# A fused top-k attention and two-stage mixture kernel: the float64 weights of the last stage are converted and split once into SBUF

## The chip, the cores and the metric

The kernel runs on one core of a Trainium2 chip. The metric is the device time of one execution in microseconds (us); lower is better. Three executions of the kernel before took 807.14, 808.33 and 810.57 us.

## The reference

```python
# attention: q, k, v are (2, 8, 576, 64), float32
scores = q @ k.T / sqrt(64)                       # 576 x 576 per batch and head
kth    = the 32nd largest score of each row       # top_k = 32
attn   = softmax of the scores >= kth, the rest left out
x      = (attn @ v), laid out as 1152 x 512       # batch and sequence by heads and head_dim

# first mixture: 4 experts, w1 (4, 512, 1024), w2 (4, 1024, 512), float32
p   = domain_probs / (domain_probs.sum(-1) + 1e-9)
out = sum over e of p[:, e] * (relu(x @ w1[e]) @ w2[e])

# second stage: w1, w2, w3 (512, 768), w_out (768, 512), float64
h      = max(out @ w1, out @ w2, out @ w3)
result = (h @ w_out).astype(float32)              # 1152 x 512
```

The four weights of the second stage are handed in as float64, as pairs of 32-bit words.

## The kernel before

The 1152 tokens are nine tiles of 128 rows, in four chunks of 2, 2, 2 and 3 tiles. `PHASES` runs the first mixture for chunks 0 to 3 and then the second stage for chunks 0 to 3. The attention makes the chunks' inputs one after another, and its work is woven into the first mixture of the earlier chunks: an outer loop steps through the attention's slots, and after each step `advance()` writes out matmul work until an estimate of TensorE's time (`clock["pe"]`) has reached a goal that grows with an estimate of VectorE's. So the program order is fixed when the kernel is written out; on the chip each engine works through its own queue in that order.

All matrix products use numbers split into two float32r parts, a high one and the rest (`product`: three matmuls for each pair of tiles). A weight of 128x1024 numbers is a unit. `w_load_to` loads it on SP's queue into one of three places `raw`; `w_split_to` (L225, L229) makes `hi` on ScalarE and `lo` by a subtraction on GpSimd, or, from chunk 3 on, on GpSimd and VectorE in turn. `hi` and `lo` have five places each, and a unit is split four units ahead of its use (`W_AHEAD`). A chunk of the first mixture uses 32 units: for each of 8 steps i, two units of the first layer (`half1`; PSUM is read by ScalarE and, L668, by VectorE) and two of the second (`half2`; the sum over experts, `acc`, is kept by VectorE, L697). `half2` of step i stands after `half1` of step i+1 in TensorE's queue. The outputs of `half2` have two PSUM places (pool `po`), so the third tile of a step can begin when VectorE has taken the first.

A chunk of the second stage uses 12 units: nine for the three first layers (`largest`, L791 keeps the maximum) and three for `w_out` (names `pso`). Before, each float64 unit is converted in four pieces of 128x256 (`to_float32`): two passes on ScalarE (L196, L197), three on VectorE (L199, L202, L205), an integer addition on GpSimd (L208), and a DMA on ScalarE's queue (L213) to a float32 copy in DRAM, `narrow`. These 48 pieces begin when the attention's slots end, one every two steps (`W_STEP`), and run beside the first mixture of chunk 3. From then on the second stage treats `narrow` like any float32 weight: for every chunk each unit is loaded and split anew, 48 loads and 48 splits. `turned` transposes a chunk's `acc` for the second stage (L745, L750, L751).

The pools of the attention (`kv`, `qp`, `at`) stay open to the end; chunk 3's hidden layer and sums take places of `kv` and `qp`.

Of the kernel before, what the change touches and what calls it, by code (L numbers as in the profile page):

```python
# [10 lines left out]
F32 = mybir.dt.float32  # L11
F32R = mybir.dt.float32r
# [7 lines left out]

# [10 lines left out]
WIDE, W_FROM, W_STEP = 4, 306, 2  # L31
# [19 lines left out]
def kernel(  # L51
# [43 lines left out]
    ms = ctx.enter_context(tc.tile_pool(name="ms", bufs=2))  # L95
    pg = ctx.enter_context(tc.tile_pool(name="pg", bufs=6, space=PSUM))
# [35 lines left out]
    def w_units():  # L132
# [21 lines left out]
        for part, c in PHASES:  # L154
            yield from (first if part == 1 else second)(c)

    dr = ctx.enter_context(tc.tile_pool(name="dr", bufs=1, space=bass.MemoryType.DRAM))
    wide = [((j, i), m[j]) for j in range(FF2 // 256) for i, m in enumerate((m1, m2, m3))]
    wide += [(j, mo[j]) for j in range(FF2 // 256)]
    narrow = {}  # L160
    for n, (key, _) in enumerate(wide):
        narrow[key] = dr.tile([P, 1024], F32, name="narrow%d" % n)
    narrow_at = {key if isinstance(key, tuple) else (key,): n for n, (key, _) in enumerate(wide)}
    narrowed = [0]
# [5 lines left out]
    def w_load_to(n):  # L170
        while w_pos["load"] < min(n, len(order)):
            key, src = order[w_pos["load"]]
            if key[1] in "cd" and narrowed[0] < WIDE * (narrow_at[key[2:]] + 1):
                return
# [5 lines left out]
    wide_raw = {}  # L180

    def wide_load(n):
        if n < WIDE * len(wide):
            wide_raw[n] = at.tile([P, 2048 // WIDE], U32, tag="s0", bufs=AHEAD_S, name="raw64")
            nc.sync.dma_start(out=wide_raw[n], in_=wide[n // WIDE][1][:, n % WIDE * 2048 // WIDE:(n % WIDE + 1) * 2048 // WIDE])

    def to_float32(n):
# [10 lines left out]
        yield True  # L198
        nc.vector.scalar_tensor_tensor(out=hf, in0=out, scalar=LEAST, in1=hf, op0=ALU.is_ge, op1=ALU.mult)  # L199
        dve(1024 // WIDE)  # L200
        yield True
        nc.vector.tensor_scalar(out=t, in0=high, scalar1=3, scalar2=0x3FFFFFF8, op0=ALU.logical_shift_left, op1=ALU.bitwise_and)  # L202
        dve(512 // WIDE)
        yield True
        nc.vector.scalar_tensor_tensor(out=t, in0=high, scalar=0xC0000000, in1=t, op0=ALU.bitwise_and, op1=ALU.bitwise_or)  # L205
        dve(1024 // WIDE)
        yield True
        nc.gpsimd.tensor_tensor(out=out.bitcast(I32), in0=out.bitcast(I32), in1=last, op=ALU.add)  # L208
        yield True
        yield True  # L210
        wide_load(n + AHEAD_S)
        yield True
        nc.scalar.dma_start(out=narrow[wide[n // WIDE][0]][:, n % WIDE * 1024 // WIDE:(n % WIDE + 1) * 1024 // WIDE], in_=out)  # L213
        narrowed[0] = n + 1

    def w_split_to(n):
        while w_pos["split"] < min(n, len(order)):
# [9 lines left out]
            late = w_pos["split"] - w_index[PHASES[LATE][1], "c" if PHASES[LATE][0] == 2 else "a", 0, 0]  # L227
            on = nc.vector if late >= 0 and late % 2 else nc.gpsimd
# [6 lines left out]
    def weight(key, oldest=None):  # L235

        w_split_to(w_index[oldest or key] + W_AHEAD)
        return w_hl[key]
# [237 lines left out]
    def attention():  # L476
# [69 lines left out]
        while s <= end:  # L546
# [20 lines left out]

# [347 lines left out]
```

## Time and profile before

| | us |
|---|---|
| median of three runs | 808.33 |
| the profiled execution, its own time | 808.2 |
| its span, first to last instruction | 806.4 |
| TensorE busy | 746.3 (93%) |
| VectorE busy | 683.8 (85%) |
| GpSimd busy | 527.2 (65%) |
| ScalarE busy | 492.7 (61%) |

The profile is of one execution. Its span leaves 1.8 us outside (808.2 against 806.4). PE is TensorE, DVE VectorE, ACT ScalarE, POOL GpSimd, SP SyncE. A row of the timeline has the start, the duration, the engine, the line of the kernel, the operation, the tiles it writes and reads, their shapes, and in brackets the idle time before it with what ended it. PE's durations overlap, since matmuls are pipelined: the distance from one start to the next is what a matmul costs.

### The profile page before, as it was taken

To read this page: it belongs to the slowest core of one execution; us is meant where nothing else is said; L and a number is where in the kernel's file an instruction comes from. 1 tells how busy PE (TensorE), PEld (TensorE's weight loads), DVE (VectorE), ACT (ScalarE), POOL (GpSimd) and SP (SyncE) were. 2 spreads that over 40 slices of the span, in tenths; PEclk is the share of its full clock that TensorE was granted. 3 is DMA by queue.
4 is the path that set the end of the run, shared out by engine and by line. 5 is a ranking of instruction groups with operands and counts; after the bars stand their busy time and mean duration, and the time that the engine had idled before them with its cause. 6 is when DMAs were issued, how large, how long until landed. Compare 5 with 4: busy or idle time off the path is not lost.

```text
span 806.4 us, 13973 instructions
## 1 busy us (share of the span) xinstructions
PE 746.3 (93%) x4942; PEld 663.2 (82%) x4942; DVE 683.8 (85%) x1242; ACT 492.7 (61%) x1027; POOL 527.2 (65%) x316
## 2 busy tenths in 40 slices
PE   3776799999999989999999999989999898999998
PEld 2454699888898879888888987879988697989996
DVE  6999989999999999999999996999999683445441
ACT  5666768677776775766777665665565444545541
POOL 2787968779888876668777685566565473555330
PEclk8556599999999999999999999999999899999999
DMA  3430245636545445253534364877777455656531
GB/s 98 117 106 13 68 131 147 190 117 173 174 137 171 135 146 151 88 169 112 161 126 146 112 188 152 270 249 250 245 251 243 157 178 167 232 165 208 178 102 40
DMA packets 50214, 126.24 MB, mean 157 GB/s; under 512 B 7904, under 2 KB 18144, under 8 KB 50144
## 3 DMA queue, kind: packets, MB, share of 16 engines
q1 hardware_dynamic: 41936, 116.69, 46.8%
q10 hardware_dynamic: 8208, 8.65, 3.1%
q8 instruction: 39, 0.64, 0.3%
q14 instruction: 31, 0.25, 0.1%
HBM read 116.67 MB, written 8.65 MB: 155 GB/s over the span
## 4 chain that ended last, share of the span: by engine, by line
DVE 41%; PE 35%; DMA 8%; issue 6%; POOL 4%; ACT 4%; SPq 2%; ACTq 0%; DVEq 0%; POOLq 0%
DVE m L370 14%; DVE work L372 13%; PE ps L588 9%; PE ps L590 9%; PE ps L589 9%; DVE p L390 6%; DMA narrow<-narrow 3%; POOL wlo L229 2%; DMA raw<-in_w_dram 2%; DVE h L668 2%; ACT whi L225 2%; SPq L246 2%; DMA kraw<-in_k_dram 1%; PE pso L590 1%; PE pso L588 1%
## 5 line engine op out<-in xcount | busy, mean ns | idle before, releaser
L229 POOL TENSOR_TENSOR wlo<-raw,whi 128x1024 fp32r<-128x1024 f32 x136 | 336.5, 2487 | 162.6 <-ACT whi L225 155.8
L225 ACT ACTIVATE whi<-raw 128x1024 fp32r<-128x1024 f32 x176 | 182.9, 1058 | 73.7 <-DMA raw<-narrow 23.8
L588 PE MATMUL ps<-xl,whi 128*128 128x256 f32 (+1 forms) x512 | 155.3, 303 | 1.7 <-DVE h L668 0.8
L370 DVE MAX8 m<-work 128x8 f32<-128x576 f32 x216 | 154.6, 742 | 0.1
L589 PE MATMUL ps<-xh,whi 128*128 128x256 f32 (+1 forms) x512 | 152.6, 298 | 0.0
L590 PE MATMUL ps<-xh,wlo 128*128 128x256 f32 (+1 forms) x512 | 152.6, 298 | 0.0
L229 DVE TENSOR_TENSOR wlo<-raw,whi 128x1024 fp32r<-128x1024 f32 x40 | 61.6, 1541 | 66.4 <-ACT whi L225 64.9
L372 DVE MATCH_REPLACE8 work<-m,work 128x576 f32<-128x576 f32 x144 | 106.4, 740 | 0.0
L588 PEld LDWEIGHTS ps<-xl,whi 128*128 128x128 f32 x512 | 99.0, 193 | 3.7 <-DVE h L668 1.3
L589 PEld LDWEIGHTS ps<-xh,whi 128*128 128x128 f32 x512 | 98.8, 193 | 0.9
L590 PEld LDWEIGHTS ps<-xh,wlo 128*128 128x128 f32 x512 | 98.7, 193 | 0.0
L590 PE MATMUL ps<-x2h,wlo 128*128 128x256 f32 (+1 forms) x288 | 85.4, 296 | 0.8 <-DVE wlo L229 0.8
L588 PE MATMUL ps<-x2l,whi 128*128 128x256 f32 (+1 forms) x288 | 85.3, 296 | 0.0
L589 PE MATMUL ps<-x2h,whi 128*128 128x256 f32 (+1 forms) x288 | 85.2, 296 | 0.0
L390 DVE SCALAR_TENSOR_TENSOR p<-s,m,p 128x576 f32<-128x576 f32 x57 | 81.0, 1422 | 0.0
L588 PE MATMUL ps<-wlo,h 128*128 128x512 f32 x192 | 77.7, 405 | 0.0
L590 PE MATMUL ps<-whi,h 128*128 128x512 f32 x192 | 75.3, 392 | 0.0
L589 PE MATMUL ps<-whi,h 128*128 128x512 f32 x192 | 75.3, 392 | 0.0
L408 PE MATMUL psp<-ident,p 128*128 128x128 f32 x288 | 50.8, 306 | 26.3 <-POOL p L394 15.4
L208 POOL TENSOR_TENSOR narrow<-narrow,raw 128x256 int32<-128x256 int32 x48 | 41.2, 858 | 44.7 <-DVE narrow L205 14.6
L349 PE MATMUL pss<-kT,ql 128*128 128x288 f32 x160 | 55.1, 358 | 13.9 <-DVE ql L293 7.6
L408 PEld LDWEIGHTS psp<-ident,p 128*128 128x128 f32 x288 | 38.3, 156 | 32.9 <-POOL p L394 18.9
(104 smaller groups left out, 1706.0 us busy)
## 6 DMA issues: line engine op xcount, KB each, us to landing
raw<-in_w_dram SPq DMA_DIRECT2D x128, 512.0 KB, 3.9
raw<-narrow SPq DMA_DIRECT2D x48, 512.0 KB, 3.8
raw<-in_m_dram SPq DMA_DIRECT2D x36, 256.0 KB, 4.4
narrow<-narrow ACTq DMA_DIRECT2D x48, 128.0 KB, 3.7
kraw<-in_k_dram SPq DMA_DIRECT2D x14, 288.0 KB, 4.5
raw<-in_mo_dram SPq DMA_DIRECT2D x12, 256.0 KB, 4.2
vt<-in_v_dram SPq DMA_DIRECT2D x8, 288.0 KB, 4.2
out_dram<-ob ACTq DMA_DIRECT2D x9, 256.0 KB, 2.0
```

Source lines behind the costliest of these rows:

```text
L208: nc.gpsimd.tensor_tensor(out=out.bitcast(I32), in0=out.bitcast(I32), in1=last, op=ALU.add)
L225: nc.scalar.activation(out=hi, in_=raw, func=AF.Copy)
L229: on.tensor_tensor(out=lo, in0=raw, in1=hi.bitcast(F32), op=ALU.subtract)
L246: nc.sync.dma_start(out=out[half * D:(half + 1) * D], in_=src)
L349: nc.tensor.matmul(ps[:, 0:SH], lhsT=l, rhs=r, start=i == 0, stop=i == len(mm) - 1)
L370: nc.vector.max(m[:, 8 * r:8 * r + 8], src)
L372: nc.vector.match_replace(out=self.w[j], in_to_replace=m[:, 8 * r:8 * r + 8], in_values=src, imm_value=NEG)
L390: nc.vector.scalar_tensor_tensor(out=p, in0=s, scalar=kth, in1=p, op0=ALU.is_ge, op1=ALU.mult, accum_out=total)
L408: nc.tensor.transpose(ps[:, r * P:(r + 1) * P], self.p[:, part, part * TAIL + r * P:part * TAIL + (r + 1) * P], ident)
L588: nc.tensor.matmul(ps, lhsT=lh, rhs=rl, start=first, stop=False)
L589: nc.tensor.matmul(ps, lhsT=lh, rhs=rh, start=False, stop=False)
L590: nc.tensor.matmul(ps, lhsT=ll, rhs=rh, start=False, stop=last)
```

## The change

- The attention's three pools are closed when its last slot is written, and a new pool `late` takes their place. Places of `late` wait tile by tile for the last use of what lay there before. Chunk 3's hidden layer and sums, which borrowed from `kv` and `qp`, move there under tags of their own (`h3`, `acc3`).
- `to_float32` becomes `to_two_parts`. The DMA to DRAM is gone. After the addition on GpSimd a piece goes on: ScalarE writes its `hi` (L212), VectorE its `lo` (L215, 128x256), into a whole unit that stays: seven units in `late`, two in places of `h` of the `hp` pool, three in `hi` and `lo` places of `wp`. The last five units wait for their places (`allowed`): two until chunk 2's first mixture is over, three until chunk 3's has split its last unit.
- The second stage reads these units directly (`weight`); its 48 loads and 48 splits are gone.
- A piece begins every three steps instead of two, for the last twelve every two, at most five are under way, and a step no longer adds the conversion's own time to the estimate of VectorE's.

The core of it:

```diff
-        out = at.tile([P, 1024 // WIDE], F32, tag="s1", bufs=AHEAD_S, name="narrow")
+        out = late[0].tile([P, PW], F32, tag="out64", bufs=STAGED, name="narrow")
...
         nc.gpsimd.tensor_tensor(out=out.bitcast(I32), in0=out.bitcast(I32), in1=last, op=ALU.add)
-        yield True
-        yield True
-        wide_load(n + AHEAD_S)
-        yield True
-        nc.scalar.dma_start(out=narrow[wide[n // WIDE][0]][:, n % WIDE * 1024 // WIDE:(n % WIDE + 1) * 1024 // WIDE], in_=out)
-        narrowed[0] = n + 1
+        wide_load(n + STAGED)
+        for _ in range(TO_HI):
+            yield True
+        while n // PARTS >= allowed[0]:
+            yield True
+        if not n % PARTS:
+            u = n // PARTS
+            pool, tag, bufs = (late[0], "w2", 2 * RESIDENT) if u < RESIDENT else (hp_, "h", 4) if u < RESIDENT + RESIDENT_H else (wp, None, 5)
+            resident[key] = [pool.tile([P, 1024], F32R, tag=tag or x, bufs=bufs, name="w" + x) for x in ("hi", "lo")]
+        hi, lo = [x[:, n % PARTS * PW:(n % PARTS + 1) * PW] for x in resident[key]]
+        nc.scalar.activation(out=hi, in_=out, func=AF.Copy)
+        yield True
+        yield True
+        nc.vector.tensor_tensor(out=lo, in0=out, in1=hi.bitcast(F32), op=ALU.subtract)
+        converted[0] = n + 1
...
+    passing.close()
+    late.append(ctx.enter_context(tc.tile_pool(name="late", bufs=1, reuse_waits="tile")))
+    for n in range(STAGED):
+        wide_load(n)
+    converting, conv, s = [], 0, 0
+    while conv < PARTS * len(wide) or converting:
+        if s >= begins[0] and conv < PARTS * len(wide) and len(converting) < STAGED:
+            converting.append(to_two_parts(conv))
+            conv += 1
+            begins[0] = s + (PART_STEP if conv < PARTS * (RESIDENT + RESIDENT_H) else LATE_STEP)
+        for x in list(converting):
+            if next(x, 0) == 0:
+                converting.remove(x)
+        clock["dve"] += PAUSE
+        keep_up()
+        s += 1
```

TensorE's queue holds the same matmuls in the same order. What moves stands on the other engines. The first place is VectorE's queue in the middle of chunk 3's first mixture, from the last `acc` of one step i on; `raw_` with a number is a piece of a float64 weight, `narrow` its result, `hl<-ps` the hidden layer's low part, `wlo<-raw` of 128x1024 the split of a unit. Before:

```order
L697 SCALAR_TENSOR_TENSOR acc<-ps_6689,gate,acc 128x512
L202 TENSOR_SCALAR narrow<-raw_6632 128x256
L205 SCALAR_TENSOR_TENSOR narrow<-raw_6632,narrow 128x256
L199 SCALAR_TENSOR_TENSOR raw_6661<-narrow,raw_6661 128x256
L202 TENSOR_SCALAR narrow<-raw_6661 128x256
L205 SCALAR_TENSOR_TENSOR narrow<-raw_6661,narrow 128x256
L199 SCALAR_TENSOR_TENSOR raw_6696<-narrow,raw_6696 128x256
L668 SCALAR_TENSOR_TENSOR hl<-ps_6725,hh 128x384
L668 SCALAR_TENSOR_TENSOR hl<-ps_6746,hh 128x384
L202 TENSOR_SCALAR narrow<-raw_6696 128x256
L229 TENSOR_TENSOR wlo<-raw,whi 128x1024
```

The same place in the changed kernel, whose lines L195, L197, L199 are L199, L202, L205 of before, L237 is L229, L669 is L668 and L698 is L697:

```order
L698 SCALAR_TENSOR_TENSOR acc<-ps_6712,gate,acc 128x512
L197 TENSOR_SCALAR narrow<-raw_6600 128x256
L199 SCALAR_TENSOR_TENSOR narrow<-raw_6600,narrow 128x256
L215 TENSOR_TENSOR wlo<-narrow,whi 128x256
L195 SCALAR_TENSOR_TENSOR raw_6648<-narrow,raw_6648 128x256
L197 TENSOR_SCALAR narrow<-raw_6648 128x256
L199 SCALAR_TENSOR_TENSOR narrow<-raw_6648,narrow 128x256
L669 SCALAR_TENSOR_TENSOR hh<-ps_6749,hh 128x384
L669 SCALAR_TENSOR_TENSOR hh<-ps_6768,hh 128x384
L215 TENSOR_TENSOR wlo<-narrow,whi 128x256
L195 SCALAR_TENSOR_TENSOR raw_6680<-narrow,raw_6680 128x256
```

Each piece now has a fourth operation here, L215, between the others.

Counted over whole steps, from the last `acc` of one step to that of the next, VectorE's queue holds in chunk 3:

| from the last `acc` of | before: L199, L202, L205, split, `acc`, `hl` | changed: the same six, then L215 |
|---|---|---|
| chunk 2, through step 0 to that of step 1 | 13, 13, 13, 6, 3, 10 | 14, 13, 14, 6, 3, 10; 14 |
| steps 2 and 3 | 10, 10, 10, 4, 6, 6 | 10, 10, 10, 4, 6, 6; 10 |
| steps 4 and 5 | 10, 10, 10, 4, 6, 6 | 11, 12, 11, 4, 6, 6; 10 |
| step 6 | 5, 5, 5, 1, 3, 2 | 2, 2, 3, 1, 3, 2; 1 |

The second place is VectorE's queue where chunk 3's first mixture ends: the last two `acc` of step 6, the transposed rows for the second stage (`x2l`), and the first `acc` of step 7. Before:

```order
L697 SCALAR_TENSOR_TENSOR acc<-ps_7573,gate,acc 128x512
L697 SCALAR_TENSOR_TENSOR acc<-ps_7592,gate,acc 128x512
L229 TENSOR_TENSOR wlo<-raw,whi 128x1024
L202 TENSOR_SCALAR narrow<-raw_7535 128x256
L751 TENSOR_TENSOR x2l<-pst,x2h 128x4x128
L205 SCALAR_TENSOR_TENSOR narrow<-raw_7535,narrow 128x256
L199 SCALAR_TENSOR_TENSOR raw_7564<-narrow,raw_7564 128x256
L202 TENSOR_SCALAR narrow<-raw_7564 128x256
L751 TENSOR_TENSOR x2l<-pst,x2h 128x4x128
L697 SCALAR_TENSOR_TENSOR acc<-ps_7630,gate,acc 128x512
```

Changed (L757 is L751):

```order
L698 SCALAR_TENSOR_TENSOR acc<-ps_7610,gate,acc 128x512
L698 SCALAR_TENSOR_TENSOR acc<-ps_7626,gate,acc 128x512
L757 TENSOR_TENSOR x2l<-pst,x2h 128x4x128
L215 TENSOR_TENSOR wlo<-narrow,whi 128x256 x5
L757 TENSOR_TENSOR x2l<-pst,x2h 128x4x128
L698 SCALAR_TENSOR_TENSOR acc<-ps_7663,gate,acc 128x512
```

The split of the second stage's first unit and four conversion steps leave this stretch, and five of the small subtractions come into it.

## Rows read from the trace of the kernel before

**Rows 1.** Busy time of each engine in stretches of the span: the stretch and its length, then PE, PEld (weight loads), DVE, ACT and POOL busy with their instructions, the granted TensorE clock (1.00 is full), the share of the DMA engines, GB/s.

```profile
500.00:550.00 50.00, 47.37 (x247) 43.38 (x246) 49.34 (x67) 31.31 (x62) 31.39 (x24) 1.00 0.82 263
550.00:600.00 50.00, 50.00 (x253) 45.04 (x252) 48.31 (x69) 28.84 (x56) 30.29 (x23) 1.00 0.76 241
600.00:650.00 50.00, 46.81 (x238) 40.87 (x237) 41.41 (x62) 25.36 (x49) 25.20 (x20) 0.93 0.65 212
700.00:750.00 50.00, 49.63 (x360) 46.86 (x359) 23.97 (x24) 25.50 (x33) 25.86 (x12) 1.00 0.56 184
```

**Rows 2.** What PE waited for between 500 us and the end: in total, times, longest.

```profile
PE ps L588 <- DVE acc L697: 5.4, 2, 3.2
PE pso L588 <- ACT h L794: 1.8, 1, 1.8
PE ps L590 <- DVE wlo L229: 0.8, 2, 0.4
PE ps L588 <- ACT acc L690: 0.4, 1, 0.4
```

**Rows 3.** The timeline of PE: two neighbouring matmuls of `half2` in chunk 3, then the first and the last of twelve after the longest wait.

```profile
569.44 0.40 PE L588 MATMUL ps<-wlo,hh 128*128 128x512 f32 x1
569.68 0.39 PE L589 MATMUL ps<-whi,hh 128*128 128x512 f32 x1
...
637.89 0.79 PE L588 MATMUL ps<-wlo,hh 128*128 128x512 f32 x1 [3.19 <-DVE acc L697]
...
642.75 0.63 PE L590 MATMUL ps<-whi,hl 128*128 128x512 f32 x1
```

**Rows 4.** The timeline of VectorE at the two splits of chunk 3 at which it waited for ScalarE.

```profile
577.78 1.23 DVE L229 TENSOR_TENSOR wlo<-raw,whi 128x1024 fp32r<-128x1024 f32 x1 [1.07 <-ACT whi L225]
...
611.26 1.23 DVE L229 TENSOR_TENSOR wlo<-raw,whi 128x1024 fp32r<-128x1024 f32 x1 [0.91 <-ACT whi L225]
```

**Rows 5.** The timeline of VectorE in stretches where nothing holds it up: the start of each row to the start of the next is the cost of the first.

```profile
594.50 0.74 DVE L697 SCALAR_TENSOR_TENSOR acc<-ps,gate,acc 128x512 f32<-128x512 f32 x1
595.16 1.21 DVE L229 TENSOR_TENSOR wlo<-raw,whi 128x1024 fp32r<-128x1024 f32 x1
596.29 0.74 DVE L697 SCALAR_TENSOR_TENSOR acc<-ps,gate,acc 128x512 f32<-128x512 f32 x1
...
601.06 1.01 DVE L668 SCALAR_TENSOR_TENSOR hl<-ps,hh 128x384 fp32r<-128x384 f32 x2
601.99 0.28 DVE L202 TENSOR_SCALAR narrow<-raw 128x256 uint32<-128x256 uint32 x1
...
620.77 0.41 DVE L199 SCALAR_TENSOR_TENSOR raw<-narrow,raw 128x256 f32<-128x256 f32 x1
621.21 0.75 DVE L202 TENSOR_SCALAR narrow<-raw 128x256 uint32<-128x256 uint32 x1
...
624.88 0.28 DVE L202 TENSOR_SCALAR narrow<-raw 128x256 uint32<-128x256 uint32 x1
625.20 0.42 DVE L205 SCALAR_TENSOR_TENSOR narrow<-raw,narrow 128x256 uint32<-128x256 uint32 x1
625.54 0.42 DVE L199 SCALAR_TENSOR_TENSOR raw<-narrow,raw 128x256 f32<-128x256 f32 x1
```

**Rows 6.** The timeline of GpSimd and of VectorE at one moment of chunk 3: a split on GpSimd, and VectorE's L202 beside it.

```profile
579.43 2.39 POOL L229 TENSOR_TENSOR wlo<-raw,whi 128x1024 fp32r<-128x1024 f32 x1 [2.77 <-ACT whi L225]
...
579.59 2.39 DVE L202 TENSOR_SCALAR narrow<-raw 128x256 uint32<-128x256 uint32 x1
```

**Rows 7.** Groups of VectorE's instructions between 491 and 643 us: line, operation, tiles and shapes, count, busy us, mean ns of one, idle time before them and what ended it.

```profile
L202 DVE TENSOR_SCALAR narrow<-raw 128x256 uint32<-128x256 uint32 x43 | 39.8, 926 | 0.7
L205 DVE SCALAR_TENSOR_TENSOR narrow<-raw,narrow 128x256 uint32<-128x256 uint32 x43 | 33.6, 781 | 1.1
L229 DVE TENSOR_TENSOR wlo<-raw,whi 128x1024 fp32r<-128x1024 f32 x17 | 24.8, 1461 | 6.6 <-ACT whi L225 6.6
L199 DVE SCALAR_TENSOR_TENSOR raw<-narrow,raw 128x256 f32<-128x256 f32 x44 | 20.6, 469 | 0.7 <-ACT narrow L196 0.7
```

**Rows 8.** The timeline of VectorE where chunk 3's first mixture begins and two steps later: the last two `acc` of chunk 2's, and the last `acc` of step 1.

```profile
503.55 1.40 DVE L697 SCALAR_TENSOR_TENSOR acc<-ps,gate,acc 128x512 f32<-128x512 f32 x2
...
545.47 0.74 DVE L697 SCALAR_TENSOR_TENSOR acc<-ps,gate,acc 128x512 f32<-128x512 f32 x1
```

**Rows 9.** The timeline of VectorE before PE's longest wait, and of ScalarE before the wait of the first `pso`.

```profile
631.23 2.59 DVE L229 TENSOR_TENSOR wlo<-raw,whi 128x1024 fp32r<-128x1024 f32 x1 [2.21 <-ACT whi L225]
...
637.10 0.73 DVE L697 SCALAR_TENSOR_TENSOR acc<-ps,gate,acc 128x512 f32<-128x512 f32 x1
...
670.29 1.06 ACT L225 ACTIVATE whi<-raw 128x1024 fp32r<-128x1024 f32 x1 [3.41 <-DMA raw<-narrow]
674.10 0.63 ACT L794 ACTIVATE h<-tm 128x512 fp32r<-128x512 f32 x1 [2.74 <-DVE tm L791]
```

**Rows 10.** The timeline at the end of the attention: SP issues the first loads of float64 pieces, PE's last product of the attention that reads `vt`, VectorE's first conversion.

```profile
480.03 1.38 SPq L185 DMA_DIRECT2D raw<-in_m_dram  x3
...
488.89 0.69 PE L454 MATMUL psv<-pt,vt 64*64 64x128 f32 x4
...
491.39 0.47 DVE L199 SCALAR_TENSOR_TENSOR raw<-narrow,raw 128x256 f32<-128x256 f32 x1 [0.69 <-ACT narrow L196]
```

**Rows 11.** DMA issues of the page: tiles, queue, count, KB each, median us from issue to landing.

```profile
raw<-in_m_dram SPq DMA_DIRECT2D x36, 256.0 KB, 4.4
```

More of the change, by code (lines that the diff above doesn't have):

```diff
@@ L154, in w_units @@
         for part, c in PHASES:
[L155 to L164, printed above, removed]
+            if part == 1:
+                yield from first(c)
     order = list(w_units())
@@ L178, in w_load_to, with to_two_parts @@
             w_pos["load"] += 1
-    wide_raw = {}
+    wide = [(("c", j, i), m[j]) for j in range(FF2 // 256) for i, m in enumerate((m1, m2, m3))]
+    wide += [(("d", j), mo[j]) for j in range(FF2 // 256)]
+    wide_raw, resident = {}, {}
+    PW = 1024 // PARTS
     def wide_load(n):
[L183 to L187, printed above, removed]
+        if n < PARTS * len(wide):
+            wide_raw[n] = late[0].tile([P, 2 * PW], U32, tag="raw64", bufs=STAGED, name="raw64")
+            nc.sync.dma_start(out=wide_raw[n], in_=wide[n // PARTS][1][:, n % PARTS * 2 * PW:(n % PARTS + 1) * 2 * PW])
+    def to_two_parts(n):
+        key = wide[n // PARTS][0]
         raw = wide_raw.pop(n).rearrange("p (n t) -> p n t", t=2)
@@ L225, in w_split_to @@
             nc.scalar.activation(out=hi, in_=raw, func=AF.Copy)
-            late = w_pos["split"] - w_index[PHASES[LATE][1], "c" if PHASES[LATE][0] == 2 else "a", 0, 0]
-            on = nc.vector if late >= 0 and late % 2 else nc.gpsimd
+            after = w_pos["split"] - w_index[PHASES[LATE][1], "a", 0, 0]
+            on = nc.vector if after >= 0 and after % 2 else nc.gpsimd
             on.tensor_tensor(out=lo, in0=raw, in1=hi.bitcast(F32), op=ALU.subtract)
@@ L645, in experts @@
         else:
-            acc = [kv.tile([P, (2 * NR + 1) * D], F32, tag="v", bufs=5, name="acc")[:, 0:DM] for _ in tiles]
+            acc = [late[0].tile([P, DM], F32, tag="acc3", bufs=len(tiles), name="acc") for _ in tiles]
         accs[c] = acc
@@ L760, in turned_ahead, with waiting_for @@
                 yield True
-    def converted(*key):
-        while narrowed[0] < WIDE * (narrow_at[key] + 1):
+    def waiting_for(*key):
+        while key not in resident or converted[0] < PARTS * ([x for x, _ in wide].index(key) + 1):
             yield None
@@ L823, with keep_up @@
     work = products()
+    def keep_up():
+        nonlocal before
+        clock["goal"] += (clock["dve"] - before) * SHARE[min(phase[0], len(SHARE) - 1)]
+        before = clock["dve"]
+        while clock["pe"] < clock["goal"]:
+            if not advance():
+                clock["pe"] = clock["goal"]
     for s, done in attention():
@@ L839 @@
                 converting.remove(x)
-        split_waiting()
-        assert not any((x.c, x.hp) in done for x in waiting)
-        x_ready.update(done)
-        clock["goal"] += (clock["dve"] - before) * SHARE[min(phase[0], len(SHARE) - 1)]
-        before = clock["dve"]
-        while clock["pe"] < clock["goal"]:
-            if not advance():
-                clock["pe"] = clock["goal"]
+        clock["dve"] += PAUSE
+        keep_up()
+        s += 1
     while advance():
```

61 lines of the change are left out of this document (27 added, 34 removed).

## Prediction

> **What bounds the kernel now.** I read first the busy time by stretches [rows 1], then what PE waited for [rows 2], then the queue that it waited for. From 500 us on PE is the bound: the span could end earlier only by PE's waits and by stretches at the lower clock. The waits are few: 5.4 us on VectorE's `acc` in two pieces, of which the longest is 3.2 and the other so 2.2, 1.8 on ScalarE's hidden layer before the first `pso`, 0.8 on splits of the second stage, 0.4 on an `acc` of ScalarE [rows 2]. After the wait of 3.19 us PE runs slower: twelve matmuls from 637.89 on stand (642.75 - 637.89)/11 = 0.44 us apart, where two of the same kind stood 0.24 apart before [rows 3], the two levels of the clock, 1.2 and 2.4 GHz; the granted clock of this stretch is 0.93 where its neighbours have 1.00 [rows 1]. That is 12 x 0.20 = 2.4 us.
>
> In the second stage VectorE and GpSimd are busy for half the time (24 and 26 of 50 us at 700 to 750 us), in chunk 3's first mixture VectorE for all of it: 49.3 and 48.3 of 50 us [rows 1]. The change takes work from the first of these and adds to the second. So the question is whether VectorE has room there.
>
> **What is removed.** 48 loads and 48 splits of the second stage go; twelve units are split once instead of four times. For PE this is worth only what it waited for. Gone are the two waits for splits (0.8), since all units but the last three lie ready, and the wait before the first `pso`: ScalarE's queue stood 3.41 us at a split whose load came back from DRAM, and the hidden layer behind it came late [rows 9]; the changed queue has no such load. The wait of 3.19 us came about in the same way: VectorE stood 2.21 us for the second stage's first split, which then took 2.59 instead of 1.21 us, so `acc` ended only at 637.83 [rows 5, 9]. In the changed order five small subtractions stand there instead, 5 x 0.34 = 1.7 us by the price below, and two `x2l`. PE has two tiles of 12 matmuls, 5.6 us at 0.23 to 0.24 us each [rows 3], before it needs that `acc`; I count this wait and the slow clock behind it as gone. Sum: 0.8 + 1.8 + 3.2 + 2.4 = **8.2 us less**. If PE still waited there, 2.6 of it would be left.
>
> **What is added.** 48 subtractions of 128x256 on VectorE (L215), 48 copies of 128x256 on ScalarE in place of 48 DMA issues (ScalarE has 20 of 50 us free [rows 1], I cost them at nothing). The prices on VectorE from start to start are: split of 128x1024 1.13, `acc` 0.66, `hl` pair 0.93, L199 0.44, L202 0.32, L205 0.34 [rows 5]. The trace has no subtraction of 128x256. L205 reads two tiles of that size, so I take its 0.34; a quarter of the split's 1.13 would be 0.28. In the changed order the subtractions do not stand in gaps: they stand between conversions and in front of `hl` and `acc`, for which PE waits.
>
> How much room is there? Between the two splits at which VectorE waited for ScalarE lie two steps of chunk 3, 611.26 - 577.78 = 33.48 us [rows 4]. The work in its queue for two steps is 10 conversions x 1.10 + 4 splits x 1.13 + 6 `acc` x 0.66 + 3 pairs x 0.93 = 11.0 + 4.5 + 4.0 + 2.8 = 22.3 us. It waited some 1.0 us [rows 4]. The other 10.2 us it was held inside instructions: L202 takes 0.28 us when free and 926 ns in the mean, L205 0.42 and 781, the split 1.21 and 1461 [rows 5, 7]; the L202 beside a GpSimd split began at 579.59 and ended with it, 0.16 us after 581.82 [rows 6]. So the room is 1 us in two steps.
>
> The changed queue, by the counts of the order, against this:
> - chunk 2's last `acc` to step 1's: 14 subtractions, one L199 and one L205 more, 14 x 0.34 + 0.8 = 5.6 us. In these 546.21 - 504.95 = 41.3 us [rows 8] PE already stood its 2.2 and 0.4 us: there is no room. All 5.6 are added.
> - steps 2 and 3: 10 subtractions, 3.4 us, less the 1.0 of room: 2.4.
> - steps 4 and 5: 10 subtractions and four conversion steps (one L199, two L202, one L205) more, 3.4 + 1.4 = 4.8, less 1.0: 3.8.
> - step 6 holds eight conversion steps fewer: VectorE catches up, but PE's lost time does not come back. The second stage has room for the rest.
>
> Sum: 5.6 + 2.4 + 3.8 = **11.8 us more**, if GpSimd holds VectorE up for as long as now, since its splits in chunk 3 stay as many. The upper end: held time grows with the work that can be held. It was 10.2 us on 15.5 us of conversions and splits, 0.66 to one; on the 5.6 + 3.4 + 4.8 = 13.8 us added that is 9.1 more, so 20.9. The lower end is nothing: the subtractions fill time in which VectorE would have been held, and PE does not notice. The nearest row is the split on VectorE, the same operation: 1461 ns against 1210, a fifth more [rows 5, 7]. A fifth of 11.8 is 2.4, so I take 14.2. PE then stands some 1 to 4 us in each step; I count no slow clock for that, since the waits of 2.2 and 0.4 left the granted clock at 1.00 [rows 1, 2]; each stand as long as 3.19 could cost up to 2.4.
>
> Sum: 14.2 - 8.2 = +6.0 us. Against the profiled execution's own time, 808.2, that is 814.2; it stands 0.1 below the median, so 814.3. **Forecast: 814 us**, 0.7% slower.
>
> Moved past queues: the loads of pieces go out on SP's queue behind the same loads as before, at 480.03 [rows 10]. They now go to places that the attention leaves.
>
> **Rivals.**
> (a) Faster: VectorE is full only because it is held. A subtraction that falls where the next conversion would have been held anyway costs nothing; this decides if under 8 of the 14 us reach PE. For it: a third of VectorE's time is held time, and it caught up with ScalarE every second step [rows 4]. Against it: its queue is in order, and it stood idle for about 1 us in 50 [rows 1]. With nothing added: 808.3 - 8.2 = 800.1. If PE's waits of 2.2 and 0.4 early in chunk 3 go too, with the DMA to DRAM: 797.5.
> (b) About even: with the 11.8 less a few us, or with 0.28 for a subtraction (34 x 0.06 = 2.0 less) and no growth of held time: +1 to +3, 809 to 812.
> (c) Held time grows in full: 20.9 - 8.2 = +12.7, 821. L202 beside a GpSimd split shows that one engine can wait for the whole of the other's instruction [rows 6]. The Trainium skill, SBUF — State Buffer, section "Who interferes with whom", says that a VectorE instruction with two SBUF inputs contends with a GpSimd instruction that reads SBUF, and that the second to issue blocks fully. By that rule every added subtraction, which has two SBUF inputs, can be held by a split of GpSimd or hold it; the trace agrees in that `hl` and `acc`, with one input in PSUM, are not among the long ones, and L205 is.
> (d) The places come late: the first pieces wait for the attention's last readers. If their loads left at 489.6, after the last product that reads `vt`, and not at 480.03, they would land 4.4 us after that [rows 11], and VectorE's first conversion would move from 491.39 to 494.0 [rows 10]: up to 2.6 us on top of the forecast, 817.
> That the change does not do what it says I exclude: the order has no load or split in the second stage.
>
> **How the numbers follow.** The forecast with (d), 811 to 819, has a chance of 0.44; (a) 0.24; (b) 0.20; (c) 0.12. A measurement can tell about 0.5%, 4 us, from no change: slower means over 812.4, faster under 804.3. Of the forecast's share about a fifth lies below 812.4. Slower: 0.35 + 0.12 = 0.47; same 0.09 + 0.20 = 0.29 and faster 0.24, of which I move 0.01 from the one to the other. The range reaches from 799, just under (a), to 823, (c) with one slow stretch of 2.4: it leaves out (a) with the early waits gone and a slower (c).
>
> **What would show it.** Right: between 500 and 640 us PE waits for VectorE's `acc` by some 10 us more in all, VectorE still busy for 48 to 50 of 50 us there, L215's mean over 0.41 us; between 640 and 805 us no wait of PE over 1 us, VectorE's and GpSimd's busy time there halved or less. Wrong: PE at 50 of 50 us through chunk 3 and VectorE with free time there. Then (a) holds, and the held time was room. If PE stands at the first `pso`, the last three units came late and the saving of 1.8 fails.

## The result, and the profile after

The changed kernel takes 818.69 us (median of four runs, 816.32 to 820.44), the kernel before 809.03 beside it; the ratio is 1.0119, 95% interval 1.0082 to 1.0155. It is slower by 1.2%. The profiled execution took 816.32 us with a span of 814.5.

The busy time by stretches, against [rows 1] (PE, PEld, DVE, ACT, POOL busy, the granted clock, DMA share, GB/s):

```profile
500.00:550.00 50.00, 42.07 (x201) 37.56 (x201) 48.93 (x75) 30.77 (x66) 29.11 (x21) 0.93 0.62 181
550.00:600.00 50.00, 44.79 (x223) 40.50 (x222) 46.94 (x71) 29.41 (x65) 26.88 (x19) 0.97 0.61 184
600.00:650.00 50.00, 46.41 (x223) 40.44 (x222) 43.87 (x68) 24.75 (x54) 25.72 (x18) 0.97 0.46 137
700.00:750.00 50.00, 50.00 (x388) 48.58 (x387) 8.20 (x13) 8.32 (x14) 5.15 (x4) 1.00 0.03 11
```

PE lost 5 us in each of the first two stretches and its clock is lower there; VectorE is as full as before. From 700 us on PE never stands, and VectorE, ScalarE and GpSimd have little left. What PE waited for from 490 us to the end, against [rows 2]:

```profile
PE ps L594 <- DVE acc L698: 10.4, 5, 3.7
PE ps L594 <- ACT acc L691: 5.3, 1, 5.3
PE ps L594 <- DVE hh L669: 1.0, 1, 1.0
```

All of it lies in chunk 3's first mixture; the waits for splits and before the first `pso` are gone. The longest wait is on ScalarE, which the prediction put at nothing. ScalarE's queue ahead of it, and the matmuls behind it on PE:

```profile
517.26 0.42 ACT L212 ACTIVATE whi<-narrow 128x256 fp32r<-128x256 f32 x1 [2.38 <-POOL narrow L201]
...
520.84 0.42 ACT L212 ACTIVATE whi<-narrow 128x256 fp32r<-128x256 f32 x1 [1.55 <-POOL narrow L201]
...
524.07 0.42 ACT L212 ACTIVATE whi<-narrow 128x256 fp32r<-128x256 f32 x1 [1.33 <-POOL narrow L201]
...
525.80 0.67 ACT L691 ACTIVATE acc<-ps,gate 128x512 f32<-128x512 f32 x1
```

```profile
526.52 0.80 PE L594 MATMUL ps<-wlo,hh 128*128 128x512 f32 x1 [5.35 <-ACT acc L691]
527.11 0.63 PE L595 MATMUL ps<-whi,hh 128*128 128x512 f32 x1
527.54 0.63 PE L596 MATMUL ps<-whi,hh 128*128 128x512 f32 x1
```

ScalarE works through its queue in order: three times its copy to `hi` (L212) waited for GpSimd's addition, 5.26 us in all, and chunk 3's first `acc` stood behind. The additions were late because of VectorE in turn. Each (L201) began 0.1 to 0.2 us after the end of VectorE's L199 of the same piece, and the L199 ahead of the second of these waits lasted about as long as a split of GpSimd beside it:

```profile
517.19 2.46 POOL L237 TENSOR_TENSOR wlo<-raw,whi 128x1024 fp32r<-128x1024 f32 x1
517.41 2.52 DVE L199 SCALAR_TENSOR_TENSOR narrow<-raw,narrow 128x256 uint32<-128x256 uint32 x1
520.06 0.74 POOL L201 TENSOR_TENSOR narrow<-narrow,raw 128x256 int32<-128x256 int32 x1 [0.42 <-POOL wlo L237]
```

Behind the wait the matmuls stand 0.43 to 0.59 us apart, and the granted clock of 526 to 532 us is 0.50, the lower of its two levels.

Where the 8.1 us between the two spans (806.4 and 814.5) lie, by the end of the last `acc` of chunk 2 and of step 5 on VectorE, the first `x2l` matmul of the second stage and PE's last matmul:

| stretch | before | after | difference |
|---|---|---|---|
| start to chunk 2's last `acc` | 504.95 | 503.61 | -1.3 |
| to the last `acc` of step 5 | 108.2 | 129.9 | +21.8 |
| to PE's first `x2l` matmul | 30.0 | 22.0 | -8.0 |
| second stage on PE | 159.4 | 155.3 | -4.1 |
| PE's last matmul to the end | 3.8 | 3.6 | -0.2 |

The first row is not the change's doing. VectorE's last softmax instruction of the attention (DVE_READ_ACCUMULATOR, L390 before, L401 after), ahead of every conversion, began at 485.46 us before and at 483.43 after; in e5 and e6 below, whose kernel is the one before up to there, it began at 487.63 and 483.05. So one execution is some 2 us ahead of another by chance, and without it the two profiled executions differ by some 10 us, like the medians (818.69 - 809.03 = 9.7).

Nearly everything else happens in the second row. One window over that stretch, of before and of after, and VectorE's groups in it (count, busy us, mean ns, idle before):

```profile
504.95:613.14 108.19, 105.56 (x532) 94.95 (x532) 104.84 (x151) 65.56 (x127) 63.89 (x50) 1.00 0.79 253
```

```profile
L202 DVE TENSOR_SCALAR narrow<-raw 128x256 uint32<-128x256 uint32 x34 | 33.9, 998 | 0.5
L205 DVE SCALAR_TENSOR_TENSOR narrow<-raw,narrow 128x256 uint32<-128x256 uint32 x33 | 24.7, 750 | 0.9
L229 DVE TENSOR_TENSOR wlo<-raw,whi 128x1024 fp32r<-128x1024 f32 x14 | 18.1, 1295 | 2.0 <-ACT whi L225 2.0
L199 DVE SCALAR_TENSOR_TENSOR raw<-narrow,raw 128x256 f32<-128x256 f32 x33 | 16.0, 485 | 0.0
```

After (L197, L199, L237, L195 are those four):

```profile
503.61:633.56 129.95, 113.21 (x540) 100.41 (x539) 124.80 (x191) 75.46 (x161) 72.17 (x51) 0.95 0.60 177
```

```profile
L197 DVE TENSOR_SCALAR narrow<-raw 128x256 uint32<-128x256 uint32 x35 | 31.4, 898 | 1.0
L195 DVE SCALAR_TENSOR_TENSOR raw<-narrow,raw 128x256 f32<-128x256 f32 x35 | 23.4, 669 | 0.0
L199 DVE SCALAR_TENSOR_TENSOR narrow<-raw,narrow 128x256 uint32<-128x256 uint32 x36 | 21.3, 591 | 0.8
L237 DVE TENSOR_TENSOR wlo<-raw,whi 128x1024 fp32r<-128x1024 f32 x14 | 19.9, 1422 | 3.4 <-ACT whi L233 3.4
L215 DVE TENSOR_TENSOR wlo<-narrow,whi 128x256 fp32r<-128x256 f32 x34 | 17.1, 502 | 0.0
```

VectorE's busy time grew by 124.80 - 104.84 = 20.0 us: the subtractions are 17.1, the splits 1.8 more, the conversions 1.5 more (76.1 against 74.6; the sums of groups count overlaps twice). Its idle time did not shrink: 129.95 - 124.80 = 5.2 us against 3.4. On PE the waits above, 16.7 us, stand where there were 2.6, 14.1 more. Its busy time in the stretch is 113.21 - 105.56 = 7.65 us longer. Of this eight matmuls more, 0.17 us apart, are 1.4 us: VectorE's last `acc` lies that much further behind PE at the end, and the next row gives it back. The rest, 6.3, is the granted clock, 0.95 in the mean instead of 1.00. Together with the waits that is 21.8.

### The profile page after: what moved, and what is told of

Same layout as the page of the kernel before. It is cut to its first block, busy times and chain, and to the rows that moved or that the text cites. A ratio compares the mean times of both kernels' runs of the same rounds, so it can differ in the third digit from the quotient of the medians.

```text
span 814.5 us, 13593 instructions
## 1 busy us (share of the span) xinstructions
PE 745.4 (92%) x4942; PEld 663.3 (81%) x4942; DVE 663.2 (81%) x1266; ACT 460.9 (57%) x1027; POOL 471.8 (58%) x292
## 4 chain that ended last, share of the span: by engine, by line
DVE 49%; PE 32%; issue 7%; ACT 4%; DMA 3%; POOL 3%; SPq 2%; POOLq 0%; ACTq 0%; DVEq 0%
DVE m L381 15%; DVE work L383 13%; PE ps L594 8%; PE ps L596 8%; PE ps L595 8%; DVE p L401 7%; DVE narrow L197 3%; DVE raw L195 2%; DVE acc L698 2%; DVE wlo L237 2%; DVE h L669 2%; POOL wlo L237 2%; SPq L257 2%; PE pso L596 2%; PE pso L594 2%
## 5 line engine op out<-in xcount | busy, mean ns | idle before, releaser
L237 POOL TENSOR_TENSOR wlo<-raw,whi 128x1024 fp32r<-128x1024 f32 x112 | 276.9, 2488 | 77.8 <-ACT whi L233 77.4
L233 ACT ACTIVATE whi<-raw 128x1024 fp32r<-128x1024 f32 x128 | 133.1, 1059 | 35.8 <-PE ps L596 15.9
L797 DVE TENSOR_TENSOR tm<-ps,tm 128x512 f32<-128x512 f32 (+1 forms) x30 | 19.1, 638 | 99.4 <-PE ps L596 99.4
L201 POOL TENSOR_TENSOR narrow<-narrow,raw 128x256 int32<-128x256 int32 x48 | 47.0, 979 | 84.0 <-DVE narrow L199 44.8
L401 DVE SCALAR_TENSOR_TENSOR p<-s,m,p 128x576 f32<-128x576 f32 x57 | 82.0, 1439 | 0.0
L419 PE MATMUL psp<-ident,p 128*128 128x128 f32 x288 | 50.1, 302 | 25.5 <-POOL p L405 13.5
```

What stands on the lines that cost most here:

```text
L233: nc.scalar.activation(out=hi, in_=raw, func=AF.Copy)
L237: on.tensor_tensor(out=lo, in0=raw, in1=hi.bitcast(F32), op=ALU.subtract)
L401: nc.vector.scalar_tensor_tensor(out=p, in0=s, scalar=kth, in1=p, op0=ALU.is_ge, op1=ALU.mult, accum_out=total)
L419: nc.tensor.transpose(ps[:, r * P:(r + 1) * P], self.p[:, part, part * TAIL + r * P:part * TAIL + (r + 1) * P], ident)
```

## The experiments

The theory: VectorE's queue is full in chunk 3, and PE goes at its pace. 1a says that the added instruction's own time decides; 1b that VectorE and GpSimd hold each other up, so that the kind of instruction decides. The rival, A, is that the pieces, their places or ScalarE come late. All ratios are to the kernel before, run on the same chip.

### e1 and e2: the subtraction taken off VectorE, and another instruction in its place

```diff
-        nc.vector.tensor_tensor(out=lo, in0=out, in1=hi.bitcast(F32), op=ALU.subtract)
+        nc.scalar.activation(out=lo, in_=out, func=AF.Copy)
+        nc.vector.max(late[0].tile([P, 8], F32, tag="top", bufs=1, name="top"), out)   # e2 alone
```

> The changed kernel with L215 taken off VectorE: the low part of a float64 weight's piece is written by ScalarE as a copy of the piece (the subtraction is left out, so the low parts are not the differences). Theory 1 (VectorE's queue is full beside chunk 3, and what the subtractions add there, own time and held time together, is what TensorE waits for): VectorE's three stretches of chunk 3, that grew from 41.3, 33.5 and 33.5 us to 50.1, 38.5 and 41.3, go back to within 2 us of the old values, TensorE's waits there to about 3 us, the median to 799 to 804. Rival A (the pieces' places and loads come late, or ScalarE's longer queue is what is late): the stretches stay long, the median at 814 or more.

> As the run with the low part copied by ScalarE, and in L215's place on VectorE a MAX8 over the same 128x256 piece, which reads one tile of SBUF and writes 128x8. Theory 1a (the subtraction's own time in the queue is the cost): the maximum takes about as long as the subtraction, so the three stretches are as long as with the subtraction less some 5 us of held time, and the median is 811 to 816. Theory 1b (the cost is mostly that a subtraction of two SBUF tiles and GpSimd's instructions hold each other up, which a maximum of one tile does not): the median is within 4 us of the run with the copy alone, 800 to 807.

e1: 803.61 us, ratio 0.9952 (0.9933 to 0.997). e2: 816.33 us, 1.0115 (1.0083 to 1.0148). Of e1, PE's waits are down to

```profile
PE ps L594 <- DVE acc L698: 4.3, 4, 1.5
PE ps L594 <- ACT acc L691: 2.9, 1, 2.9
```

By the ratios the 48 subtractions cost (1.0119 - 0.9952) x 808 = 13.5 us, and places and loads are not late without them: A falls, as far as it means these. PE's waits did not go to the 3 us that were expected, and VectorE's three stretches are 45.8, 34.4 and 36.8 us, of which only the second is within 2 us of the old values. The MAX8, with one SBUF input, costs 816.33 - 803.61 = 12.7 us, which looked like 1a. It was the wrong reading, as e6 and e11 show. In e2 the MAX8 itself is never held (419 ns), but L197 and L195 take longer than in e1 (616 and 578 ns there), as long as in the changed kernel, and L199 and the splits less long (581 against 772, 1490 against 1673 ns): 3.5 us more in sum, so that most of the cost is the MAX8's own time. At 492 to 640 us:

```profile
L197 DVE TENSOR_SCALAR narrow<-raw 128x256 uint32<-128x256 uint32 x40 | 36.3, 906 | 1.1
L195 DVE SCALAR_TENSOR_TENSOR raw<-narrow,raw 128x256 f32<-128x256 f32 x40 | 27.0, 676 | 0.0
...
L216 DVE MAX8 top<-narrow 128x8 f32<-128x256 f32 x36 | 15.1, 419 | 0.0
```

### e3: pieces every four steps

```diff
-PARTS, PART_STEP, LATE_STEP, STAGED, TO_HI = 4, 3, 2, 5, 4
+PARTS, PART_STEP, LATE_STEP, STAGED, TO_HI = 4, 4, 2, 5, 4
```

> The changed kernel with a piece of the first nine units begun every four steps instead of three (PART_STEP 4), nothing else. VectorE's queue then holds 8 instead of 10 or 11 conversions in two steps of chunk 3, 22.6 us of work with the subtractions at 0.34, against 22.3 in the kernel before and 25.7 to 27.1 in the changed one; 14 conversions instead of 6 are left for the second stage's first chunk. Theory 1: TensorE's waits in chunk 3 fall to 2 to 6 us, against 16.7; in the second stage's first chunk up to 5 us of new waits; the median is 802 to 809. Rival A (places, loads or ScalarE late): no gain, 815 or more.

807.06 us, 0.9998 (0.9979 to 1.0018). Chunk 3 is back at PE's pace; the waits move to the second stage, where 14 pieces are still to be converted, and the granted clock at 650 to 700 us is 0.90:

```profile
PE pso L594 <- DVE wlo L215: 5.6, 4, 2.5
PE ps L594 <- DVE acc L698: 1.4, 2, 0.7
```

### e4 and e8: work moved from VectorE to GpSimd

```diff
-        nc.vector.tensor_tensor(out=lo, in0=out, in1=hi.bitcast(F32), op=ALU.subtract)
+        nc.gpsimd.tensor_tensor(out=lo, in0=out, in1=hi.bitcast(F32), op=ALU.subtract)   # e4
...
-            on = nc.vector if after >= 0 and after % 2 else nc.gpsimd
+            on = nc.vector if after >= 0 and after % 4 == 3 else nc.gpsimd               # e8
```

> The changed kernel with the 48 small subtractions (L215) on GpSimd instead of VectorE. They cost GpSimd about 0.75 us each, 36 us, of which it has the room (it was busy for 27 to 29 of 50 us beside chunk 3). Theory 1a (VectorE's own time decides): the median falls to 800 to 806. Theory 1b (the two engines hold each other up, whoever subtracts): GpSimd's subtractions hold VectorE's conversions for 0.55 us each, as its additions do, and the median stays at 812 to 820.

> The changed kernel, of whose 128x1024 splits in chunk 3 VectorE makes every fourth instead of every second; the other eight go to GpSimd at about 2.5 us each. 1a: VectorE's queue is shorter by 8 x 1.13 to 8 x 1.41 us, 9 to 11 us, so 806 to 811 and PE's waits for acc in chunk 3 fall from some 17 us to 6 to 9; the 128x256 instructions on VectorE keep their means. 1b (GpSimd's work holds VectorE's two-input instructions): the eight splits on GpSimd hold VectorE by as much as they free, the means of the 128x256 instructions rise, 815 to 822. Rival: GpSimd comes late with its splits and PE waits for wlo: over 818.

e4: 817.52 us, 1.0119 (1.0072 to 1.0166): no better than the change, though VectorE was busy for only 42.28 of 50 us at 550 to 600 us, where the changed kernel has 46.94. e8: 822.72 us, 1.0188 (1.017 to 1.0205): 4 us worse, where 1a wanted 9 to 11 us better. VectorE's groups of e8 at 492 to 640 us:

```profile
L197 DVE TENSOR_SCALAR narrow<-raw 128x256 uint32<-128x256 uint32 x38 | 38.7, 1020 | 1.1
L199 DVE SCALAR_TENSOR_TENSOR narrow<-raw,narrow 128x256 uint32<-128x256 uint32 x38 | 27.7, 729 | 0.9
...
L237 DVE TENSOR_TENSOR wlo<-raw,whi 128x1024 fp32r<-128x1024 f32 x7 | 10.0, 1422 | 0.9 <-ACT whi L233 0.8
```

Splits of 14 us left VectorE (24.0 us there in the changed kernel, 10.0 here), and the 128x256 instructions that stayed took 9 us more, though they are fewer. 1a alone is refuted: most of the time that went to GpSimd came back on VectorE. The rival of the expectation, that PE waits for GpSimd's splits, is out: PE waited 11.8 us for `acc` of VectorE, 2.9 for `acc` of ScalarE and 2.0 for the hidden layer, never for `wlo`. What made e4 no better and e8 worse is not shown in full: VectorE had time free in both (at 550 to 600 us it was busy for 42.65 of 50 us in e8), PE's waits in e8 are as long as in the changed kernel, 16.7 us, and the granted clock is lower, 0.90 at 550 to 600 us instead of 0.97.

### e5 and e6: one instruction more in the kernel before

```diff
         nc.gpsimd.tensor_tensor(out=out.bitcast(I32), in0=out.bitcast(I32), in1=last, op=ALU.add)
...
         wide_load(n + AHEAD_S)
+        nc.vector.tensor_tensor(out=extra, in0=out, in1=out, op=ALU.subtract)   # e5
+        nc.vector.max(extra, out)                                               # e6 instead
```

> The kernel before with one more VectorE subtraction of 128x256 for each of the 48 pieces, after GpSimd's addition (a piece minus itself into a place that nobody reads), and nothing else of the change: loads, splits and DRAM copies stay. 1a (the own time of one more instruction per piece in VectorE's full queue decides): some 41 of the 48 lie in chunk 3's first mixture; the step from the copy on ScalarE to the MAX8 in its place cost 12.7 us in the changed kernel, so 10 to 16 us here: 818 to 825 where the kernel before gives 808 to 809, and PE's waits for VectorE's acc in chunk 3 grow from 5 to about 15 us. Rival, VectorE's held time gives way (the subtraction falls where VectorE would have been held): 0 to 3 us, 808 to 812.

> The same place, but the added VectorE instruction is a MAX8 over the 128x256 piece, with one SBUF input and eight numbers written. 1a: the same time as the subtraction within 3 us, 817 to 825. 1b (only an instruction with two SBUF inputs is held by GpSimd and holds it): at most 4 us over the kernel before, 808 to 813, while the subtraction costs 10 or more.

e5: 823.82 us, 1.0199 (1.018 to 1.0219). e6: 809.37 us, 1.0019 (1.0 to 1.0037). Here the kind of instruction decides, 16 us against 1.5. Three rows of e5 and e6 at 492 to 640 us:

```profile
L212 DVE TENSOR_TENSOR extra<-narrow 128x256 f32<-128x256 f32 x39 | 41.7, 1069 | 0.0
```

```profile
L202 DVE TENSOR_SCALAR narrow<-raw 128x256 uint32<-128x256 uint32 x42 | 30.3, 722 | 0.0
...
L212 DVE MAX8 extra<-narrow 128x8 f32<-128x256 f32 x41 | 17.1, 417 | 0.0
```

The subtraction takes 1069 ns in the mean, where L205 of the same size takes 0.42 us when nothing holds it [rows 5]. The MAX8 takes its 417, and L202, which took 926 ns without it [rows 7], takes 722. The MAX8 runs while GpSimd's addition runs, when L202 behind it would have been held anyway.

The Trainium skill, SBUF — State Buffer, section "Who interferes with whom", says that a VectorE instruction with at most one SBUF input does not contend with GpSimd unless it is in a two-port mode, that one with two SBUF inputs contends with GpSimd's reads, and that `tensor_scalar` can enter a two-port mode. The runs agree: MAX8 417 to 419 ns in the means of e2, e6 and e11, the subtraction up to 1069, and L202, a TENSOR_SCALAR with one input, from 0.28 us free [rows 5] to a mean of 998.

### e10 and e11: two neighbours change places

Why then did the same MAX8 cost 12.7 us in e2? In e2 it stood ahead of L195, and GpSimd's addition began in its second half. One more `yield` lets it change places with L195 and moves nothing else of note in VectorE's queue: in each of the steps 2 to 5 it holds as many conversions, splits and MAX8 as e2, to within one of each kind. Theory 2, formed from e5 and e6, stands in the expectation of e10. e10 does that with the subtraction of the changed kernel, e11 with the MAX8 of e2:

```diff
         yield True
         yield True
+        yield True
         nc.vector.tensor_tensor(out=lo, in0=out, in1=hi.bitcast(F32), op=ALU.subtract)   # e10; the MAX8 in e11
```

> The changed kernel with the subtraction of each piece one step later: on VectorE it changes places with its neighbour, L199, L195, L215, L197 instead of L199, L215, L195, L197. GpSimd starts its addition L201 some 0.3 us after L199's end, so the subtraction now stands beside that addition instead of ahead of it. Theory 2 (VectorE's queue sets chunk 3's pace; an instruction that GpSimd can't hold costs nothing beside an instruction of GpSimd, one that it can hold costs its time anywhere): the subtraction has two SBUF inputs, so it is held in L197's place (mean 0.9 to 1.0 us instead of 0.50, L197 down by 0.4 to 0.5) and the time stays at 815 to 821. Theory 1a (own time alone): the same time, with the means as they were. If the place alone decides, whatever the instruction: 804 to 810.

> The kernel with ScalarE's copy and the MAX8 in the subtraction's place (low parts left as copies), and the MAX8 one step later, so that on VectorE it changes places with L195. Nothing else is moved. Theory 2: the MAX8, which GpSimd doesn't hold (417 to 420 ns in each run so far), now runs beside GpSimd's addition and takes time in which L197 was held: L197 falls from 0.91 to some 0.5 to 0.6 us, and the time from 816 to 804 to 809, as in the kernel before, where the MAX8 behind its neighbour cost 1.5 us. Theory 1a (an instruction costs its own 0.34 us wherever it stands in a full queue): 814 to 818, as without the swap.

e10: 817.73 us, 1.0136 (1.0105 to 1.0166), no gain. e11: 808.39 us, 1.002 (1.0 to 1.0041), 8 us less than e2 for a swap of neighbours. First e2, VectorE, then e11, VectorE and GpSimd, at one piece each. In e2 GpSimd's addition began at 573.67:

```profile
573.46 0.41 DVE L216 MAX8 top<-narrow 128x8 f32<-128x256 f32 x1
573.80 0.91 DVE L195 SCALAR_TENSOR_TENSOR raw<-narrow,raw 128x256 f32<-128x256 f32 x1
```

```profile
576.75 0.41 DVE L195 SCALAR_TENSOR_TENSOR raw<-narrow,raw 128x256 f32<-128x256 f32 x1
577.09 0.41 DVE L217 MAX8 top<-narrow 128x8 f32<-128x256 f32 x1
577.43 0.53 DVE L197 TENSOR_SCALAR narrow<-raw 128x256 uint32<-128x256 uint32 x1
```

```profile
577.07 0.75 POOL L201 TENSOR_TENSOR narrow<-narrow,raw 128x256 int32<-128x256 int32 x1 [2.55 <-ACT hh L669]
```

In e11 L195 is done when the addition begins, the MAX8 runs beside it, and L197 is held for only the rest; its mean falls from 906 to 502 ns, as expected. L199's rose from 581 to 836 and the splits' from 1490 to 1766, so not all is regained: by the ratios to the kernel before e11 is still (1.002 - 0.9952) x 808 = 5.5 us over e1, which has no MAX8, where e2 is 13.2 over it. In e10 the subtraction's mean went from 0.50 to 0.66 us and L197's from 916 to 847, in the expected directions but by a third and a sixth of the expected sizes. Its time is the one that both theory 2 and 1a expected; it rules out only that the place alone decides. Against 1a stand e6 and e11. So theory 2 holds in the main: an instruction that GpSimd doesn't hold costs little beside an instruction of GpSimd (1.5 us in e6, 5.5 in e11) and its time elsewhere; the subtraction costs its time in either place.

### e7, e9 and e12: the pace of the pieces

The work can't be made to vanish, but it can be spread: fewer pieces beside steps 0 to 4, the rest later, but not so late as in e3.

```diff
-            begins[0] = s + (PART_STEP if conv < PARTS * (RESIDENT + RESIDENT_H) else LATE_STEP)
+            begins[0] = s + ((4 if conv < 20 else 3) if conv < 36 else 1)    # e7
+            begins[0] = s + (4 if conv < 28 else 1)                          # e9, and TO_HI = 2
+            begins[0] = s + ((4 if conv < 26 else 3) if conv < 36 else 1)    # e12
```

> The changed kernel with its pieces begun every four steps for the first twenty, every three up to the 36th and every one for the last twelve. In chunk 3 this puts 19 subtractions and 21 conversions beside steps 0 to 3 where the changed kernel has 25 and 28, and 37 and 40 of the 48 are done when the first mixture ends (35 and 39 in step 5, 41 and 42 at the end in the changed kernel; 32 and 34 with four steps all the way). 1a: waits of PE in chunk 3 of at most 4 us, no wait for the last pieces in the second stage (5.6 us with four steps all the way), so the changed kernel's saving of 8 to 12 us is left over: 798 to 803, faster than the kernel before by 0.6 to 1.3%. Rival (places or ScalarE late, not VectorE's queue): 812 to 818, the first long wait on ScalarE's acc stays. If the middle of the pieces still comes too late for w_out: 804 to 807 with a wait at pso.

> The changed kernel with a piece every four steps for the first 28 and every one after that (at most five under way), and hi two steps earlier behind GpSimd's addition. Steps 0 to 4 of chunk 3 hold 23 subtractions and 25 conversions instead of 30 and 33, step 6 takes 9 and 7 instead of 1 and 2, and all but two of the 48 are done when the second stage's third unit is reached. Theory 1 or 2: the stretches to step 5 stay near those of four steps all the way (42.5, 17, 16, 17, 16) and steps 5 and 6, with fewer splits, take the rest for 1 to 4 us of waits; no wait at pso: 798 to 803, 0.6 to 1.2% faster than the kernel before. If VectorE comes late in step 6 by as much as the 9 subtractions and 7 conversions cost (some 12 us against 16 us of the step): 804 to 809, with a wait for acc of over 3 us at 630 to 650.

> The changed kernel with a piece every four steps for the first 26, every three up to the 36th and every one for the last twelve; hi stays four steps behind GpSimd's addition. Steps 0 to 4 of chunk 3 are those of four steps all the way (23 subtractions and 25 conversions), steps 5 and 6 hold 9 and 10 instead of 7 and 8, and at the second stage's first stretch 4 more pieces are done (38 conversions against 34), which at some 2 us a piece is more than the 5.6 us for which PE waited for the last pieces there. VectorE's queue as the bound: stretches between the last acc of successive steps near 42.5, 17, 16, 17, 16 to 17, 15 to 16, no wait over 1 us at pso, 799 to 804, 0.4 to 1.0% faster than the kernel before. If the last pieces still come late for pso: 804 to 807, a wait there of 1 to 4 us. If steps 5 and 6 are too full: 805 to 810, an acc wait of over 2.5 us at 610 to 640.

e7: 805.4 us, 0.996 (0.9941 to 0.9978), over the expected 798 to 803: 7.6 us of waits for VectorE's `acc` instead of at most 4, in a profiled execution of 808.98 us, the slowest of twelve. The time is the one expected for pieces that come late, but there is no wait at `pso`. e9: 816.26 us, 1.0105 (1.0076 to 1.0134), outside both expectations. Its waits:

```profile
PE ps L594 <- DVE acc L698: 10.2, 3, 7.3
PE ps L594 <- ACT acc L691: 3.7, 1, 3.7
```

The 7.3 us are one wait for an `acc` in step 6 behind a bunch of conversions in VectorE's queue. The other is on ScalarE again, with `hi` closer behind GpSimd's addition, but e9 changed two things at once.

e12: 798.4 us (798.09 to 801.11), ratio 0.9891 (0.9865 to 0.9916), just under the expected 799 to 804, faster than the kernel before by 1.1% and, by the ratios, than the changed one by (1.0119 - 0.9891) x 808 = 18 us:

```profile
500.00:550.00 50.00, 48.05 (x251) 44.26 (x250) 47.27 (x71) 31.71 (x64) 29.62 (x20) 1.00 0.64 202
550.00:600.00 50.00, 49.36 (x250) 44.61 (x250) 47.84 (x69) 30.11 (x62) 30.39 (x21) 1.00 0.57 179
600.00:650.00 50.00, 47.62 (x267) 42.47 (x266) 45.59 (x84) 26.48 (x66) 22.46 (x19) 1.00 0.41 123
```

```profile
PE ps L594 <- DVE acc L698: 4.6, 4, 1.7
PE ps L594 <- ACT acc L691: 0.4, 1, 0.4
```

It does all that the change does. Its waits for `acc` are at most 1.7 us, the clock is 1.00, there is no wait at `pso`, and its second stage takes 155.3 us on PE like that of the changed kernel.

## Why the prediction was right, step by step

**Sign and size.** Forecast were 814 us, 0.7% slower, range 799 to 823; measured 818.69 and 1.2%, 9.7 us more than the kernel before beside it, where 6.0 were forecast. The profiled execution's own time, 814.2 forecast and 816.32 measured, is nearer than that because it was 2.0 us ahead before the change began. That the sum came so near is in part luck: too little was removed in it and too little added.

**What is removed.** The waits for splits and at `pso` are gone, 2.6 us forecast; the second stage on PE is 4.1 shorter, 1.5 us beyond these waits, and why was not looked for. The wait of 3.19 us and the slow clock behind it are gone, 5.6 forecast: from PE's first matmul of step 7 to its first `x2l` it took 31.85 us before (611.32 to 643.17) and 25.62 after (629.97 to 655.59), 6.2 less. With the 0.2 at the end that is 10.5, where 8.2 were forecast.

**What is added.** The mechanism was right, PE waiting for work of VectorE; the term was too small. From PE's first matmul of chunk 3 to its first of step 7 it took 111.9 us before (499.38 to 611.32) and 132.4 after (497.56 to 629.97): 20.5 more, where 14.2 were forecast. PE's waits are 14.1 of this. The other 6.4 are the lower clock, and the step that failed is "I count no slow clock". It rested on a wait of 2.21 us that had left the clock at 1.00; here a wait of 2.04 us was followed by 0.72 over 606 to 612 us, one of 3.74 by 0.72 over 586 to 592, and the one of 5.35 by 0.50. Seen from VectorE it is one lateness: its busy time grew by 20.0 us and it had 5.2 us free in 130, so at the full clock PE might have stood that much longer. That is argued from the rows and was not tried.

Within VectorE's queue the price of 0.34 us with a fifth more was about right. From start to start, the prediction's unit, the 34 subtractions took 14.4 us, 0.42 each; their mean of 0.50 counts the overlap with the next instruction. The held time of the conversions did not grow (2.23 us a piece before, 2.16 after). The splits took 1.8 us more, and the room of 1.0 us in two steps was not used: VectorE's idle time rose by 1.8 instead.

**ScalarE at nothing.** The copies' own time costs nothing that shows (e1 has a second copy for each piece and is faster), but the first of them wait for GpSimd, which came late behind VectorE, and the longest wait of all, 5.35 us, is behind them. With pieces every four steps at first it is at most 0.5 us (e7, e12); what of that is the pace and what the distance to GpSimd's addition was not taken apart.

**Rivals.** (a) A subtraction that falls where VectorE would be held costs nothing: refuted for the subtraction (e5 and e10); for the MAX8 nearly so in e6 and in part in e11. (b) The even case did not come. (c) The time of 821 came within 2.3 us, and the rule behind it holds for the subtraction (e5 against e6); but the held time did not grow in full. (d) is out: the first pieces were loaded at 477.99 instead of 480.03, and VectorE's first conversion began at 489.37 instead of 491.39 [rows 10], both ahead by the 2.0 us of the whole execution and no more.

**What would show it.** PE's waits for VectorE's `acc` are 10.4 us; before they were 5.4 [rows 2], or 2.2 without the one that was to go, so 8.2 more instead of "some 10". L215's mean 0.50, over 0.41. No wait of PE after 640 us, and VectorE's and GpSimd's busy time at 700 to 750 down to a third and a fifth. VectorE was 44 to 49 of 50 us busy, a little under the 48 to 50.

## What to carry to other kernels

Look at what shares a full engine's queue before moving work into the stage that it paces: here the removal was worth some 10 us and the same change cost some 20 where it was put, and only another pace (every four steps, then three, then one) made 1.2% slower into 1.1% faster. Price a VectorE instruction with two SBUF inputs by what it takes in that stage beside GpSimd, not by its free time; moving work to GpSimd did not shorten the time (e4, e8). An instruction that GpSimd does not hold, here the MAX8, costs little if it stands right where GpSimd's instruction runs.

## What the runs showed of the hardware

- Beside GpSimd L197, a TENSOR_SCALAR with one SBUF input, was stretched most, from 0.28 us free to 1020 ns in the mean (e8), and a MAX8 over the same 128x256 never: each of the 48 took 408 to 430 ns in e2, e6 and e11.
- Two neighbours in one queue, swapped, were worth 8 us of 816 (e2 and e11).
- PE's stands of 1.7 us and less left the granted clock at 1.00 (e12). Behind a stand of 5.35 us it was 0.50 over 6 us, behind 3.74 us 0.72 (the changed kernel), and 0.90 over 50 us in e3 with four stands of 5.6 us in all. The length of one stand does not tell: 2.21 us in the kernel before left it at 1.00, and behind 2.04 us in the changed kernel it was 0.72 over 6 us.
